# Float64 half units: one load shape and more staging slots, and the w_out remainder taken on VectorE

## The chip, the cores and the metric

The kernel runs on one core of a Trainium2 chip. The metric is the device time of one execution in microseconds (us); three executions of the kernel before took 1278.87, 1280.46 and 1280.32 us, median 1280.32 us.

## The reference

Three layers run one after the other, on 8 batches of 576 rows (4608 rows of 512 values):

```python
a = softmax(phi)                                   # 576 x 32 per head
k_m, v_m = einsum('bhsm,bhsd->bhmd', a, k), einsum('bhsm,bhsd->bhmd', a, v)
attn = softmax(q @ k_m.T / sqrt(64))
x = attn @ v_m                                     # layer 1, 4608 x 512
h = x @ moe_w_in                                   # layer 2, 512 -> 2048
x = (h * sigmoid(1.702 * h)) @ moe_w_out           # 2048 -> 512
e = argmax(x @ w_gate)                             # layer 3, one of 8 experts per row
out = gate * sigmoid(x @ w_output_gate)[e] * (relu(x @ w1[e]) @ w2[e])
```

The weights `moe_w_in` and `moe_w_out` arrive in float64. They are handed to the chip as their raw 64-bit words, and the kernel itself turns them into float32.

## The kernel before, in words

**Units and half units.** Layer 2's 2048 hidden values are cut into 16 units of 128. A unit has two half units of 128 rows by 512 float64 values (512 KB): one of `w_in`, one of `w_out`. There are `NV` = 32 half units. `conv_load(n)` brings half unit n into a staging tile on the SyncE queue (SP); it reads from the second byte pair on, so that the 16-bit pieces fall where the arithmetic wants them. Read so, the very last half unit would reach one piece past the end of the array. It is therefore loaded as 127 rows and one short row, by two DMAs (L181 and L183); the other 31 are one DMA of 128 rows each.

**Conversion.** `conv_slot(n)` converts half units n and n+1, so there are 16 conversions, those of `w_in` (n = 0, 4, ...) and of `w_out` (n = 2, 6, ...) in turn. Each is two ScalarE (ACT) calls (L195) that take the top pieces, then nine VectorE (DVE) instructions (L196 to L212) that put exponent and fraction together. For `w_out` the result is also split in two: ScalarE rounds it to fp32r (L214) and GpSimd (POOL) subtracts that from the value (L215), which leaves the remainder. Matmuls on TensorE (PE) are done three times with such pairs (`mm3`: high by high, high by low, low by high). For `w_in` the split comes later: `project` multiplies the unit by the attention's values on PE (L341), and ScalarE and VectorE split the product (L345, L346).

**Where half units wait.** Half units 0 to 11 land in four slots of the tile `wb` of weight group 2 (group 2's weights are converted later), the others in the pool `stg` with 3 buffers. `stg` also serves k and v of batches 2 to 7 and layer 3's weights. A load stands in SP's program behind the conversion that empties its slot.

**Steps.** The program is a list of steps: a step is one unit for one half batch (288 columns), that is 6 matmuls into `h`, the activation on ACT and DVE (L367 to L370), and 12 matmuls into four accumulators `acc`. The first 24 steps run units 0 to 5 for four half batches; each part sum goes to DRAM by `ev` (L387) and `partd` (L704). Then units 6 to 15 follow for the first half batch (steps 24 to 33), whose end is L393, where the part sum is added; by then all 16 conversions must be done. From there no weight of layer 2 is converted any more: the other half batches, layer 2 for batches 2 to 7, and layer 3 with its routing.

**Order.** Each engine runs its instructions in program order. Conversions are called at a fixed pace against the steps (`PB + j * PR`), or earlier where a step needs them; a scheduler then lays out each engine's order. The attention of batch 1 (`compress`, `query`) is spread over steps 0 to 12; its k and v lie in five chunks in `wb` of weight group 3, and its q is loaded by `load_q` on the same SP queue.

Of the kernel before, what the change touches and what calls it, by code (L numbers as in the profile page):

```python
# [10 lines left out]
F32 = mybir.dt.float32  # L11
F32R = mybir.dt.float32r
U32 = mybir.dt.uint32
I32 = mybir.dt.int32
U16 = mybir.dt.uint16
# [15 lines left out]
NF1, NF2 = 16, 8  # L31
SLOT = 128
# [5 lines left out]
OUT_SHAPE = (N, DM)  # L38
CH = [(0, 128), (128, 128), (256, 128), (384, 128), (512, 64)]
LOOK = 2  # L40
LEAD = 8
FE = 60
CV0 = (0, 4, 8)
NR, NT = 12, 24
O1, R1, OQ, RQ, OR, RR = 0, 0.5, 6, 0.4, 9, 0.6
S1 = 32
ORDER = 'p k0 k1 c0 k2 k3 c1 k4 q0 c2 w q1'
# [5 lines left out]
def tile_kernel(ctx: ExitStack, tc: tile.TileContext, phiT, kv, qT, w1, w2, wg, out):  # L53
    nc = tc.nc
    PS = bass.MemoryType.PSUM
    w1 = w1.bitcast(U16).rearrange("u a p n -> (u a p n)")

    const = ctx.enter_context(tc.tile_pool(name="const", bufs=1))
    sb = ctx.enter_context(tc.tile_pool(name="sb", bufs=2))
# [74 lines left out]
    def stage(g, slot, n=1024):  # L134
        a, b = group(g, "stage")
        t, o = (b, slot) if slot < 6 else (a, slot - 6)
        return t.rearrange("p u n -> p (u n)")[:, int(1024 * o):int(1024 * o) + n]
# [10 lines left out]
    def load_kv(b, c):  # L148
        s0, n = CH[c]
        if b < 2:  # L150
            t = stage(2, 6) if (b, c) == (0, 4) else stage(3, c)
        else:
            t = sb.tile([128, 1024], F32, name="stg", bufs=3)
        nc.sync.dma_start(out=t[:n], in_=kv[b, s0:s0 + n])
        kv_t[b, c] = t

# [11 lines left out]
    NV = 2 * NF1  # L168
    raw_t = {}
    loaded = [3]  # L170

    def conv_load(n):


        if n < NR:
            raw_t[n] = stage(2, 2 + n % 4).bitcast(U16)
        else:
            raw_t[n] = sb.tile([128, 2048], U16, name="stg", bufs=3)
        o = (2 * (2 * (n // 4) + n % 2) + n % 4 // 2) * 128 * 2048 + 1
        rows = 128 if n < NV - 1 else 127  # L180
        nc.sync.dma_start(out=raw_t[n][:rows], in_=w1[o:o + rows * 2048].rearrange("(p n) -> p n", p=rows))  # L181
        if rows < 128:
            nc.sync.dma_start(out=raw_t[n][rows:, :2047], in_=w1[o + rows * 2048:o + 128 * 2048 - 1].rearrange("(p n) -> p n", p=1))  # L183

    def conv_slot(n):


        if n < NT:
            top, t = (stage(3, 5 + (n + i) % 6 / 2, 512).bitcast(U16) for i in range(2))
        else:  # L190
            top, t = (sb.tile([128, 1024], U16, name=("phi0", "phi1", "c0")[(n + i) % 3], bufs=1) for i in range(2))
        raw = [raw_t.pop(n + i) for i in range(2)]
        tops = [x.rearrange("p (n b) -> p n b", b=4)[:, :, 2] for x in raw]
        for i in range(2):
            nc.scalar.activation(out=t.bitcast(BF16)[:, 512 * i:512 * i + 512], in_=tops[i].bitcast(BF16), func=AF.Abs)  # L195
        nc.vector.tensor_scalar(out=t.bitcast(BF16), in0=t.bitcast(BF16), scalar1=WLO, scalar2=WHI,  # L196
                                op0=ALU.max, op1=ALU.min)
        nc.vector.tensor_scalar(out=t, in0=t, scalar1=3, scalar2=0x3FFF,
                                op0=ALU.logical_shift_left, op1=ALU.bitwise_and)
        for i in range(2):  # L200
            h = slice(512 * i, 512 * i + 512)
            nc.vector.scalar_tensor_tensor(out=top[:, h], in0=tops[i], scalar=0xC000, in1=t[:, h],
                                           op0=ALU.bitwise_and, op1=ALU.bitwise_or)
        nc.vector.tensor_scalar(out=t, in0=top, scalar1=0xFF80, scalar2=None, op0=ALU.bitwise_and)
        for i in range(2):
            h = slice(512 * i, 512 * i + 512)
            u = 2 * (n // 4) + i
            wa, wb = (x[:, u % 4] for x in group(u // 4, "A"))
            m = raw[i].bitcast(U32).rearrange("p (n b) -> p n b", b=2)[:, :, 0]
            w = wa if n % 4 < 2 else m.bitcast(F32)  # L210
            nc.vector.scalar_tensor_tensor(out=w, in0=m, scalar=2.0 ** -36, in1=t.bitcast(BF16)[:, h], op0=ALU.mult, op1=ALU.mult)
            nc.vector.tensor_add(out=w, in0=w, in1=top.bitcast(BF16)[:, h])  # L212
            if n % 4 >= 2:
                nc.scalar.copy(out=wb[:, 512:1024], in_=w)  # L214
                nc.gpsimd.tensor_sub(out=wb[:, 1024:1536], in0=w, in1=wb[:, 512:1024].bitcast(F32))  # L215
                u_t[u] = (wb[:, 0:256], wb[:, 256:512]), (wb[:, 512:1024], wb[:, 1024:1536])
        while loaded[0] < min(NV, n + (6 if n + 5 < NR else 5)):
            conv_load(loaded[0])
            loaded[0] += 1

    d_reg = {}
    stg_t = {}

    def load2(key, src):
        stg_t[key] = sb.tile([128, 1024], F32, name="stg", bufs=3)
        nc.sync.dma_start(out=stg_t[key], in_=src)

    def split2(key, slot):
# [354 lines left out]
    def slot_tasks():  # L583
# [39 lines left out]
        def g(i):  # L623
            p = misc([128, 4, SLOT], 1 - i)
            for j in range(4):
                nc.tensor.transpose(p[:, j], st["h"][:, i, j], ident)
            t = sb.tile([128, 2, 4, SLOT], F32R, name="stg", bufs=3)
            nc.scalar.copy(out=t[:, 0], in_=p)
            nc.vector.tensor_sub(out=t[:, 1], in0=p, in1=t[:, 0].bitcast(F32))
            st["g", i] = t  # L630
# [50 lines left out]
    def spread(step, thunks, every=1):  # L681
        for i, t in enumerate(thunks):
            put(int(step + i * every), t)
# [50 lines left out]
    def attn_tasks():  # L734
        for b in range(B):
            s0 = S1 if b == 1 else start["A", b, 0]
            if b:
                q1 = query(b, 1)
                q1.insert(2, lambda b=b: load_q(b + 1, 0) if b + 1 < B else None)
                if b == 1:  # L740
                    spread(OR, q1, RR)
                else:
                    spread(s0 + 1, q1, 2)
            if b + 1 < B:
                n = b + 1
                cm = compress(n)
                q0 = query(n, 0)
                q0.insert(2, lambda n=n: load_q(n, 1))
                if b:
                    put(s0 + 1, lambda n=n: load_phi(n))  # L750
                    for c in range(3):
                        put(s0 + 2, lambda n=n, c=c: load_kv(n, c))
                    o = s0 + 8
                    put(o + 4, lambda n=n: load_kv(n, 3))
                    put(o + 5, lambda n=n: load_kv(n, 4))
                    spread(o, cm)
                    spread(o + 10, q0, 2)
                else:
                    put(O1, lambda n=n: load_phi(n), lambda n=n: load_q(n, 0))
                    for c in range(5):  # L760
                        put(O1, lambda n=n, c=c: load_kv(n, c))
                    spread(O1, cm, R1)
                    spread(O1 + OQ, q0, RQ)

    def project_tasks():
        place = {x[:4]: i for i, x in enumerate(steps)}
        for b in range(1, B):
            for u, n in ((0, 4), (4, 2), (6, 2), (8, 4), (12, 4)) if b == 1 and CUT % 4 else ((0, 4), (4, 4), (8, 4), (12, 4)):
                need, prev = place["A", b, 0, u] - LOOK, place["A", b - 1, 1, u + n - 1] - LOOK
                assert prev < need  # L770
                put(max(prev, need - LEAD), lambda b=b, u=u, n=n: project(b, u, n))

# [37 lines left out]
    done = [0]  # L810
# [33 lines left out]
    put(1, setup2)  # L844
    for i in range(-LOOK, n_steps):
        j = i + LOOK
        if j < n_steps:
# [29 lines left out]
def host(q, k, v, phi, moe_w_in, moe_w_out, moe2_w_gate, moe2_w_output_gate, moe2_w1, moe2_w2):  # L877
    import numpy as np
    c = np.ascontiguousarray
    phiT = c(phi.reshape(B, 2, 4, S, M).transpose(0, 1, 2, 4, 3).reshape(B, 2, 128, S))  # L880
    kvp = np.empty((B, S, H, 2 * D), np.float32)
    kt, vt = k.transpose(0, 2, 1, 3), v.transpose(0, 2, 1, 3)
    kvp[:, :, 0::2, :D] = vt[:, :, 0::2]
    kvp[:, :, 0::2, D:] = kt[:, :, 0::2]
    kvp[:, :, 1::2, :D] = kt[:, :, 1::2]
    kvp[:, :, 1::2, D:] = vt[:, :, 1::2]
    q6 = q.reshape(B, 4, 2, 2, HS, D)[:, :, ::-1]
    qTp = c(q6.transpose(0, 3, 2, 5, 1, 4).reshape(B, 2, 128, 4, HS))

    def units(wi, wo):  # L890
        f = wi.shape[1] // 128
        a = wi.reshape(KD, 128, f, 128).transpose(2, 1, 0, 3).reshape(f, 128, 512)
        return np.concatenate([a, wo.reshape(f, 128, 512)], axis=2)

    w1 = c(units(moe_w_in, moe_w_out).reshape(NF1, 128, 2, 512).transpose(0, 2, 1, 3)).view(np.int64)
    w2 = c(np.stack([units(moe2_w1[e], moe2_w2[e]) for e in range(E)]))
    wg = c(np.concatenate([moe2_w_gate, moe2_w_output_gate], axis=1).reshape(KD, 128, 16).transpose(1, 0, 2))
    return dict(phiT=phiT, kv=kvp.reshape(B, S, H * 2 * D), qT=qTp, w1=w1, w2=w2, wg=wg)
# [21 lines left out]
```

## Time and profile before

| | before |
|---|---|
| median of three executions | 1280.32 us |
| the profiled execution | 1287.78 us, span 1286.1 us |
| PE busy | 1196.4 us (93%) |
| DVE busy | 742.4 us (58%) |
| ACT busy | 497.7 us (39%) |
| POOL busy | 133.9 us (10%) |
| mean granted TensorE clock | 0.963 |

A share here is a mean over the whole span. The engines are limited by different things in the first 210 us, where weights are converted, and behind them, so the rows of each stretch are read apart.

### The profile page before, as it was taken

How to read it: one execution, taken by the hardware profiler on the slowest of the kernel's cores; microseconds unless marked ns; L12 is line 12 of the kernel's file. 1: busy time of each engine (PE TensorE's matmuls, PEld its weight loads, DVE VectorE, ACT ScalarE, POOL GpSimd, SP SyncE). 2: the span in 40 equal slices, each digit the busy share in tenths (PEclk: the TensorE clock that was granted, in tenths of full speed). 3: DMA queues.
4: the chain of work that ended last, by engine and by line, in shares of the span. 5: the costliest groups of instructions: out<-in, count | busy, mean ns of one | idle time of the engine just before them, and what ended most of it. 6: DMA issues, size and time to landing. Idle time of an engine off the chain costs nothing. (4 is left out here: it accounts for less than half of the span.)

```text
span 1286.1 us, 24689 instructions
## 1 busy us (share of the span) xinstructions
PE 1196.4 (93%) x9628; PEld 1107.5 (86%) x9628; DVE 742.4 (58%) x2011; ACT 497.7 (39%) x1144; POOL 133.9 (10%) x137
## 2 busy tenths in 40 slices
PE   4689737999999999999999999999999999999996
PEld 2478626888988988999889889989999999999995
DVE  5898726576466467466556546676463553544521
ACT  3445414344444444443443444553242332332410
POOL 1221000020100100101101102001110001001100
PEclk8689967999999999999999999999999999999998
DMA  8534313433311311401311310475453443534300
GB/s 297 193 107 122 131 63 95 126 80 88 108 42 56 112 39 56 130 20 56 130 38 38 119 31 20 107 230 150 130 162 95 136 156 85 171 103 123 116 23 22
DMA packets 77017, 132.00 MB, mean 103 GB/s; under 512 B 12738, under 2 KB 49730, under 8 KB 76898
## 3 DMA queue, kind: packets, MB, share of 16 engines
q1 hardware_dynamic: 75170, 130.25, 33.2%
q8 instruction: 76, 1.25, 0.4%
q14 instruction: 43, 0.35, 0.1%
q0 software_dynamic: 1728, 0.15, 0.1%
HBM read 99.65 MB, written 31.12 MB: 102 GB/s over the span
## 5 line engine op out<-in xcount | busy, mean ns | idle before, releaser
L352 PE MATMUL acc<-g,wb 128*128 128x288 f32 x4608 | 690.1, 298 | 13.5 <-ACT wb L214 6.2
L352 PEld LDWEIGHTS acc<-g,wb 128*128 128x128 f32 x4608 | 642.6, 191 | 22.1 <-ACT g L369 6.8
L352 PE MATMUL h<-x,wb 128*128 128x288 f32 x2560 | 478.0, 305 | 36.6 <-DVE g L370 24.2
L352 PEld LDWEIGHTS h<-x,wb 128*128 128x128 f32 x2560 | 386.4, 191 | 86.1 <-issue 30.7
L367 ACT ACTIVATE th<-h 128x288 f32<-128x288 f32 x256 | 105.0, 411 | 122.0 <-PE h L352 121.4
L352 PE MATMUL h<-x,wa 128*128 128x288 f32 x512 | 151.5, 296 | 0.0
L369 ACT CAST g<-th 128x288 fp32r<-128x288 f32 x196 | 84.9, 433 | 171.2 <-PE acc L352 149.0
L370 DVE TENSOR_TENSOR g<-th,g 128x288 fp32r<-128x288 f32 x196 | 88.8, 453 | 100.2 <-ACT g L369 99.9
L368 DVE SCALAR_TENSOR_TENSOR th<-th,h 128x288 f32<-128x288 f32 x196 | 87.8, 448 | 75.5 <-ACT th L367 74.6
L373 DVE SCALAR_TENSOR_TENSOR g<-h,g 128x288 fp32r<-128x288 f32 x128 | 58.0, 453 | 117.3 <-ACT g L372 116.9
L231 ACT CAST wb<-stg 128x1024 fp32r<-128x1024 f32 x72 | 75.6, 1050 | 105.5 <-PE acc L352 90.4
L372 ACT ACTIVATE g<-h 128x288 fp32r<-128x288 f32 x128 | 52.2, 408 | 162.9 <-PE acc L352 162.0
L352 PEld LDWEIGHTS h<-x,wa 128*128 128x128 f32 x512 | 96.8, 189 | 0.0
L232 DVE TENSOR_TENSOR wa<-stg,wb 128x512 fp32r<-128x512 f32 x72 | 51.5, 715 | 77.4 <-ACT wb L231 76.9
L578 POOL TENSOR_TENSOR rt<-rt,scl 128x1152 f32<-128x1152 f32 x15 | 33.6, 2241 | 352.5 <-DVE rt L404 252.4
L330 POOL TENSOR_TENSOR x<-sf,x 128x288 fp32r<-128x288 f32 x32 | 25.9, 808 | 420.7 <-ACT x L329 394.4
L514 POOL DMA_INDIRECT listd<-ids,pos x48 | 45.5, 948 | 188.8 <-DVE ssm L321 67.4
L233 DVE TENSOR_TENSOR wb<-stg,wb 128x512 fp32r<-128x512 f32 x72 | 57.0, 792 | 0.0
L341 PE MATMUL m<-wa,kvc 64*32 64x512 f32 (+1 forms) x592 | 42.2, 576 | 10.7 <-DVE wa L212 9.3
L346 DVE TENSOR_TENSOR wb<-m,wb 128x512 fp32r<-128x512 f32 (+1 forms) x74 | 42.3, 608 | 15.7 <-ACT wb L345 15.7
L345 ACT CAST wb<-m 128x512 fp32r<-128x512 f32 (+1 forms) x74 | 35.6, 529 | 17.9 <-PE m L341 17.7
L369 ACT CAST g<-h 128x288 fp32r<-128x288 f32 x60 | 23.9, 398 | 46.6 <-PE acc L352 30.0
(200 smaller groups left out, 811.1 us busy)
## 6 DMA issues: line engine op xcount, KB each, us to landing
stg<-in_w_dram SPq DMA_DIRECT2D x91, 512.0 KB, 4.0
stg<-in_kv_dram SPq DMA_DIRECT2D x24, 512.0 KB, 4.0
x2d<-x SPq DMA_DIRECT2D x16, 576.0 KB, 5.9
x2tok<-rt SPq DMA_DIRECT2D x64, 144.0 KB, 2.9
x<-x2d SPq DMA_DIRECT2D x16, 576.0 KB, 4.0
out_dram<-rt SPq DMA_DIRECT2D x64, 144.0 KB, 2.8
q<-in_qT_dram SPq DMA_DIRECT2D x15, 576.0 KB, 3.9
wb<-in_w_dram SPq DMA_DIRECT2D x12, 512.0 KB, 4.8
```

The lines of the kernel that those rows point to most:

```text
L231: nc.scalar.copy(out=wb[:, 0:1024], in_=stg)
L232: nc.vector.tensor_sub(out=wa, in0=stg[:, 0:512], in1=wb[:, 0:512].bitcast(F32))
L233: nc.vector.tensor_sub(out=wb[:, 1024:1536], in0=stg[:, 512:1024], in1=wb[:, 512:1024].bitcast(F32))
L346: nc.vector.tensor_sub(out=lo, in0=p[e], in1=hi.bitcast(F32))
L352: nc.tensor.matmul(p, lhsT=w[a][:, c0:c0 + 128], rhs=x[c], start=(first and i == 0), stop=(last and i == 2))
L367: nc.scalar.activation(out=t, in_=p, func=AF.Tanh, scale=0.851)
L368: nc.vector.scalar_tensor_tensor(out=o, in0=t, scalar=1.0, in1=p, op0=ALU.add, op1=ALU.mult)
L369: nc.scalar.copy(out=g[:, 0], in_=o)
L370: nc.vector.tensor_sub(out=g[:, 1], in0=o, in1=g[:, 0].bitcast(F32))
L372: nc.scalar.activation(out=g[:, 0], in_=p, func=AF.Relu)
L373: nc.vector.scalar_tensor_tensor(out=g[:, 1], in0=p, scalar=0.0, in1=g[:, 0].bitcast(F32), op0=ALU.max, op1=ALU.subtract)
L514: nc.gpsimd.indirect_dma_start(out=listd, out_offset=bass.IndirectOffsetOnAxis(ap=st["pos"][:, c:c + 1], axis=0), in_=ids[:, 2 * b * NJ + ...
```

## The change

The array is handed over flat and with one 64-bit word more at its end, so that the last half unit can be read as 128 rows by one DMA like the others. `stg` has 4 buffers in place of 3. Half units 12 to 15 land in the slots of group 2 as well, 16 to 19 in the four slots of group 3 in which k and v of batch 1 lay, and 20 to 31 in `stg`. Loads beyond half unit 15 are held until step 5 of the program (`free`), and then called for up to half unit 23 at once, later six ahead of the conversion. And the remainder of `w_out` (L215) is subtracted on VectorE.

```diff
+NS = 4
-NR, NT = 12, 24
+NR, NT = 16, 24
...
-            t = sb.tile([128, 1024], F32, name="stg", bufs=3)
+            t = sb.tile([128, 1024], F32, name="stg", bufs=NS)
...
         if n < NR:
             raw_t[n] = stage(2, 2 + n % 4).bitcast(U16)
+        elif n < NR + 4:
+            raw_t[n] = stage(3, n % 4).bitcast(U16)
         else:
-            raw_t[n] = sb.tile([128, 2048], U16, name="stg", bufs=3)
+            raw_t[n] = sb.tile([128, 2048], U16, name="stg", bufs=NS)
         o = (2 * (2 * (n // 4) + n % 2) + n % 4 // 2) * 128 * 2048 + 1
-        rows = 128 if n < NV - 1 else 127
-        nc.sync.dma_start(out=raw_t[n][:rows], in_=w1[o:o + rows * 2048].rearrange("(p n) -> p n", p=rows))
-        if rows < 128:
-            nc.sync.dma_start(out=raw_t[n][rows:, :2047], in_=w1[o + rows * 2048:o + 128 * 2048 - 1].rearrange("(p n) -> p n", p=1))
+        nc.sync.dma_start(out=raw_t[n], in_=w1[o:o + 128 * 2048].rearrange("(p n) -> p n", p=128))
...
                 nc.scalar.copy(out=wb[:, 512:1024], in_=w)
-                nc.gpsimd.tensor_sub(out=wb[:, 1024:1536], in0=w, in1=wb[:, 512:1024].bitcast(F32))
+                nc.vector.tensor_sub(out=wb[:, 1024:1536], in0=w, in1=wb[:, 512:1024].bitcast(F32))
...
-        while loaded[0] < min(NV, n + (6 if n + 5 < NR else 5)):
+        conv_loads(n + 6)
+
+    def conv_loads(n):
+
+        while loaded[0] < (min(NV, max(n, NR + 4 + NS)) if "free" in raw_t else min(n, NR)):
             conv_load(loaded[0])
             loaded[0] += 1
...
                     spread(O1, cm, R1)
+                    put(O1 + 5, lambda: raw_t.update(free=True), lambda: conv_loads(done[0] + 4))
                     spread(O1 + OQ, q0, RQ)
...
-    w1 = c(units(moe_w_in, moe_w_out).reshape(NF1, 128, 2, 512).transpose(0, 2, 1, 3)).view(np.int64)
+    w1 = units(moe_w_in, moe_w_out).reshape(NF1, 128, 2, 512).transpose(0, 2, 1, 3).reshape(-1)
+    w1 = np.concatenate([w1, w1[:1]]).view(np.int64)
```

In the order of the instructions the change shows at three places. Line numbers of the kernel after are up to 6 higher than those of before (L183 there is L181 here, L708 is L704, L155 is L154). On SP, the loads of half units 20 to 31 (`stg<-in_w_dram`) between the stores of the part sums (`partd`) stand so before:

```order
L181 DMA stg<-in_w_dram 128x2048 x4
L704 DMA partd_0_104<-ev 128x1152
L181 DMA stg<-in_w_dram 128x2048 x4
L704 DMA partd_1_105<-ev 128x1152
L181 DMA stg<-in_w_dram 128x2048 x4
L181 DMA stg<-in_w_dram 127x2048
L183 DMA stg<-in_w_dram 1x2047
L154 DMA stg<-in_kv_dram 128x1024
```

and so after:

```order
L708 DMA partd_1_103<-ev 128x1152
L708 DMA partd_0_104<-ev 128x1152
L183 DMA stg<-in_w_dram 128x2048 x4
L708 DMA partd_1_105<-ev 128x1152
L183 DMA stg<-in_w_dram 128x2048 x4
L155 DMA stg<-in_kv_dram 128x1024 x2
```

Behind the last part sum 4 loads are left in place of 5 and a short one, all of one shape; 8 stand behind the third part sum, where 9 and the short one stood.

On SP again, from the end of batch 1's k and v (`wb_119`, group 3) to batch 1's second q, the order was before (`wb_123` are the slots of group 2):

```order
L154 DMA wb_119<-in_kv_dram 64x1024
L120 DMA listd<-x_525 128x288
L181 DMA stg<-in_w_dram 128x2048 x2
L181 DMA wb_123<-in_w_dram 128x2048 x2
L181 DMA stg<-in_w_dram 128x2048 x3
L704 DMA partd_0_102<-ev 128x1152
L162 DMA q<-in_qT_dram 128x1152
```

and is after:

```order
L155 DMA wb_119<-in_kv_dram 64x1024
L121 DMA listd<-x_525 128x288
L183 DMA stg<-in_w_dram 128x2048 x3
L183 DMA wb_123<-in_w_dram 128x2048 x2
L183 DMA stg<-in_w_dram 128x2048
L183 DMA wb_123<-in_w_dram 128x2048 x2
L183 DMA wb_119<-in_w_dram 128x2048
L183 DMA wb_123<-in_w_dram 128x2048 x2
L183 DMA wb_119<-in_w_dram 128x2048 x3
L708 DMA partd_0_102<-ev 128x1152
L163 DMA q<-in_qT_dram 128x1152
```

Fourteen loads (half units 10 to 23) stand ahead of the first part sum's store and of that q, in place of seven (10 to 16); four of them go into the slots from which batch 1's k and v are read.

On DVE, the last conversion (half units 30 and 31) stood so before:

```order
L196 TENSOR_SCALAR phi_1719<-phi_1719 128x1024
L198 TENSOR_SCALAR phi_1719<-phi_1719 128x1024
L368 SCALAR_TENSOR_TENSOR h<-th,h 128x288
L202 SCALAR_TENSOR_TENSOR phi_1718<-stg,phi_1719 128x512 x2
L370 TENSOR_TENSOR g<-h,g 128x288
L204 TENSOR_SCALAR phi_1719<-phi_1718 128x1024
L368 SCALAR_TENSOR_TENSOR h<-th,h 128x288
L211 SCALAR_TENSOR_TENSOR stg<-stg,phi_1719 128x512 x2
L212 TENSOR_TENSOR stg<-stg,phi_1718 128x512 x2
L370 TENSOR_TENSOR g<-h,g 128x288
```

and stands so after (L372 and L374 there are L368 and L370 here, L350 is L346):

```order
L196 TENSOR_SCALAR phi_1710<-phi_1710 128x1024
L350 TENSOR_TENSOR wb_1439<-m_1726,wb_1439 128x2x128
L198 TENSOR_SCALAR phi_1710<-phi_1710 128x1024
L350 TENSOR_TENSOR wb_1439<-m_1727,wb_1439 128x2x128
L202 SCALAR_TENSOR_TENSOR phi_1709<-stg,phi_1710 128x512 x2
L372 SCALAR_TENSOR_TENSOR h<-th,h 128x288
L204 TENSOR_SCALAR phi_1710<-phi_1709 128x1024
L372 SCALAR_TENSOR_TENSOR h<-th,h 128x288
L211 SCALAR_TENSOR_TENSOR stg<-stg,phi_1710 128x512 x2
L212 TENSOR_TENSOR stg<-stg,phi_1709 128x512 x2
L374 TENSOR_TENSOR g<-h,g 128x288
L215 TENSOR_TENSOR wb_1439<-stg,wb_1439 128x512 x2
```

The two subtractions L215 follow the conversion with one other instruction between; seven more such pairs stand behind the other conversions of `w_out`.

## Rows read from the trace of the kernel before

**Rows 1.** The page: busy tenths of PE in 40 slices of the span.
```profile
PE   4689737999999999999999999999999999999996
```

**Rows 2.** Stretches: busy us of PE, PEld, DVE, ACT, POOL (instructions); clock, DMA share, GB/s.
```profile
17.00:146.00 129.00, 100.92 (x786) 81.41 (x787) 114.50 (x255) 61.05 (x146) 23.98 (x20) 0.81 0.46 157
146.00:208.00 62.00, 29.20 (x183) 24.88 (x182) 28.02 (x57) 15.10 (x34) 5.12 (x4) 0.70 0.30 96
208.00:1286.00 1078.00, 1058.79 (x8590) 997.45 (x8588) 595.81 (x1675) 415.63 (x954) 102.23 (x91) 1.00 0.32 94
...
174.00:196.00 22.00, 5.34 (x44) 3.38 (x44) 1.15 (x3) 1.55 (x4) 0.00 (x0) 0.58 0.13 48
```

**Rows 3.** Timeline: start, length, instruction [idle before it <- what ended that].
```profile
17.00 0.43 DVE L196 TENSOR_SCALAR wb<-wb 128x1024 bf16<-128x1024 bf16 x1 [7.34 <-ACT wb L195]
...
168.48 0.67 ACT L195 ACTIVATE c<-stg 128x512 bf16<-128x512 bf16 x1 [3.75 <-DMA stg<-in_w_dram]
...
195.76 0.65 ACT L195 ACTIVATE phi<-stg 128x512 bf16<-128x512 bf16 x1 [19.39 <-DMA stg<-in_w_dram]
196.45 0.43 DVE L196 TENSOR_SCALAR phi<-phi 128x1024 bf16<-128x1024 bf16 x1 [19.57 <-ACT phi L195]
...
199.33 1.09 PE L352 MATMUL h<-x,wb 128*128 128x288 f32 x3 [18.95 <-DVE g L370]
...
208.06 0.86 DVE L393 SCALAR_TENSOR_TENSOR x<-acc,x 128x288 f32<-128x288 f32 x2 [0.53 <-PE acc L352]
```

**Rows 4.** Timeline of SP's queue, the last weight loads.
```profile
172.65 0.31 SPq L181 DMA_DIRECT2D stg<-in_w_dram  x1
173.01 8.59 SPq L183 DMA_DIRECT2D stg<-in_w_dram  x1
```

**Rows 5.** DMA: rate in 40 slices of 184 to 195 us; issues, KB each, us to landing.
```profile
GB/s 328 209 60 30 30 30 15 30 30 15 30 30 30 15 30 30 30 15 30 30 30 15 30 30 15 30 30 30 15 30 30 30 15 30 30 15 30 30 30 15
...
stg<-in_w_dram SPq DMA_DIRECT2D x19, 512.0 KB, 5.2
```

**Rows 6.** DVE to 210 us by line and form: busy us, mean ns of one.
```profile
L323 DVE TENSOR_TENSOR sa<-sa,ssm 128x288 f32<-128x288 f32 x8 | 5.3, 684 | 0.0
...
L212 DVE TENSOR_TENSOR wa<-wa,wa 128x512 f32<-128x512 f32 x8 | 5.1, 682 | 0.0
...
L198 DVE TENSOR_SCALAR wa<-wa 128x1024 uint16<-128x1024 uint16 x8 | 5.0, 625 | 0.1
...
L313 DVE TENSOR_TENSOR sa<-sa,smx 128x288 f32<-128x288 f32 x8 | 3.3, 449 | 0.0
...
L211 DVE SCALAR_TENSOR_TENSOR wa<-wb,wa 128x512 f32<-128x512 uint32 x4 | 3.2, 836 | 0.0
...
L198 DVE TENSOR_SCALAR wb<-wb 128x1024 uint16<-128x1024 uint16 x4 | 1.7, 420 | 0.1
```

**Rows 7.** POOL to 215 us: busy us, mean ns of one, idle before it.
```profile
L215 POOL TENSOR_TENSOR wb<-stg,wb 128x512 fp32r<-128x512 f32 x10 | 13.3, 1350 | 91.7 <-ACT wb L214 91.7
L215 POOL TENSOR_TENSOR wb<-wb,wb 128x512 fp32r<-128x512 f32 x6 | 9.4, 1581 | 26.9 <-ACT wb L214 26.9
L330 POOL TENSOR_TENSOR x<-sf,x 128x288 fp32r<-128x288 f32 x8 | 6.4, 800 | 53.8 <-ACT x L329 27.6 <-DMA q<-in_qT_dram 26.2
```

**Rows 8.** Waits of DVE from 43 to 146 us: us in total, times, longest.
```profile
DVE h L368 <- ACT th L367: 6.4, 6, 2.7
DVE wa L196 <- ACT wa L195: 2.6, 2, 1.3
```

**Rows 9.** Timeline near 70 us, a remainder on ACT and POOL.
```profile
69.56 1.27 ACT L214 CAST wb<-wb 128x512 fp32r<-128x512 f32 x2 [2.21 <-DVE wb L212]
...
70.32 4.05 POOL L215 TENSOR_TENSOR wb<-wb,wb 128x512 fp32r<-128x512 f32 x2 [10.32 <-ACT wb L214]
```

**Rows 10.** Timelines of SP's queue and PE: batch 1's second q and its first use.
```profile
84.19 0.33 SPq L162 DMA_DIRECT2D q<-in_qT_dram  x1
...
92.53 0.72 PE L306 MATMUL m<-q,kvc 64*32 64x288 f32 x16
```

More of the change, by code (lines that the diff above doesn't have):

```diff
@@ L55, in tile_kernel @@
     PS = bass.MemoryType.PSUM
-    w1 = w1.bitcast(U16).rearrange("u a p n -> (u a p n)")
+    w1 = w1.bitcast(U16)
     const = ctx.enter_context(tc.tile_pool(name="const", bufs=1))
@@ L224, in load2 @@
     def load2(key, src):
-        stg_t[key] = sb.tile([128, 1024], F32, name="stg", bufs=3)
+        stg_t[key] = sb.tile([128, 1024], F32, name="stg", bufs=NS)
         nc.sync.dma_start(out=stg_t[key], in_=src)
@@ L626, in g @@
                 nc.tensor.transpose(p[:, j], st["h"][:, i, j], ident)
-            t = sb.tile([128, 2, 4, SLOT], F32R, name="stg", bufs=3)
+            t = sb.tile([128, 2, 4, SLOT], F32R, name="stg", bufs=NS)
             nc.scalar.copy(out=t[:, 0], in_=p)
```

## The prediction

> **What bounds the kernel now.** I read the page's slices first. PE is 90% busy or more from the eighth slice on, but not in the first seven, some 225 us, and slices five and six fall to 7 and 3 tenths [rows 1]. A cut by stretches says what each part hangs on [rows 2]. From the first conversion on DVE at 17.0 us [rows 3] to 146 us, DVE is busy for 114.5 of 129 us and PE for 100.9 at a mean clock of 0.81: that stretch is DVE's. From 146 to 208 us, where L393 ends the second pass over the first half batch [rows 3], both are idle for more than half of the time: PE 29.2 and DVE 28.0 of 62 us. From 208 us on PE is busy for 1058.8 of 1078 us at full clock, and nothing there is worth having for a change that ends with the conversions. So the question is when L393 runs. All later work follows it with PE as its bound, and the end moves as L393 moves.
>
> Why is the middle stretch empty? The timeline shows one chain [rows 3]: ACT's L195 sits idle for 19.39 us for a load into `stg`, DVE's L196 for 19.57 behind it, PE for 18.95 behind DVE. That load is the last half unit, issued at 172.65 us, its short row at 173.01 [rows 4]. From 186 to 195 us the transfer rate lies flat at 15 to 30 GB/s with nothing else moving; the 128-row loads of the same size have a median of 5.2 us from issue to landing [rows 5]. The 127-row load took 195.76 - 172.65 = 23.1 us. A smaller wait of 3.75 us, also for a load, stands in front of the conversion before [rows 3].
>
> **The change part by part.**
>
> *The last load as 128 rows.* At 5.2 us it would land at 172.65 + 5.2 = 177.9 us, not 195.8: 17.9 us off the chain, if nothing else moved.
>
> *More slots.* Before, loads 17 to 31 wait for `stg` slots one conversion at a time. After, eight loads are left behind the third part sum, the rest having been issued earlier, as the order shows. I expect ACT's L195 to wait for no load behind 43 us. That removes the 3.75 us above and DVE's 2.6 us between 43 and 146 us [rows 8]. At worst (slots come free no earlier than the loads are wanted) it removes nothing. Once L393 is past, the fourth buffer has nothing to win: PE is idle for 19.2 us in 1078 [rows 2]. The extra word of the array adds no instruction.
>
> *The remainder on DVE.* Sixteen subtractions of 128x512 are added to DVE. The nearest row is L212, the same shape, two operands in SBUF: 682 ns [rows 6], so 16 x 0.682 = 10.9 us. POOL loses 13.3 + 9.4 = 22.7 us [rows 7], which nobody waited for much. What DVE gets back is the stretch that POOL put on its instructions: L198 takes 625 ns on average in its first group and 420 in the second (8 x 0.205 = 1.6 us), L323 684 where its like L313 takes 449 (8 x 0.235 = 1.9), L211's slow group 836 against 682 (4 x 0.154 = 0.6): 4.1 us [rows 6]. L330 stays on POOL with 6.4 us, so I give L215 its share of POOL's time, 22.7 of 29.1: 3.2 us. Bounds: nothing, if the stretch is L330's, and 4.1.
>
> A page of the Trainium skill would give more: "SBUF — State Buffer", section "SBUF: two separate sides", says that GpSimd and VectorE share a pair of ports which one instruction holds alone, so that the other blocks, also where VectorE has two operands in SBUF. By it up to 22.7 us of DVE could come back and the subtractions would be free. The rows agree only in part: two L215 took 4.05 us near 70 us instead of twice 1.3 to 1.6 [rows 7, 9], so there POOL was the one that stood still.
>
> *A new wait.* DVE runs in order, and L215 needs ACT's rounding L214. The order puts one instruction of DVE between the conversion and L215. Two L214 take 1.27 us and begin as the first half is done [rows 9], so a pair of L215 can hold DVE for something between 0 and 1.27 us, eight times: 0 to 10 us. Queued behind it are L370, which PE's next 12 matmuls wait for, and the next conversion. L368 or the like covers some 0.4 us, and the first L214 starts early; I take 0.4 us a pair, 3 us.
>
> *The sum.* DVE's work from 17 to L393 was 114.5 + 28.0 = 142.5 us [rows 2]. After: 142.5 + 10.9 - 3.2 = 150.2. From 17 to 146 us DVE was idle for 14.5 us, 2.6 of it for loads [rows 8]; without these it was busy for 114.5 of 126.4 us, 90.6%. The rest of the idle time is the latency of ACT and PE (L368 for L367, 6.4 us, is the largest [rows 8]), and stays. 150.2 / 0.906 = 165.8, with the new wait 168.8 us, so L393 starts at 17.0 + 168.8 = 185.8 us instead of 208.1: 22.3 us less. A second way keeps the middle stretch's own pace: take out the waits for loads there (19.57 on DVE and the 3.75 us) and add 10.9 - 3.2 + 3 = 10.7 us of DVE, none of it hidden: 12.6 us; with half hidden in the idle time, 18. The first way lets the conversions fill DVE's idle time, which the order supports: the conversions of half units 22 to 29 stand one to three activations earlier than before. I take 21 us, nearer to the first. PE also ran at a mean clock of 0.70 in the middle stretch and at 0.58 from 174 to 196 us [rows 2]; with no long idle time it should be granted full speed, which is what lets PE follow DVE there.
>
> The profiled execution took 1287.8 us, 7.5 above the median of the three runs; I take the same 21 us off both: 1266.8 for a profiled execution and 1280.3 - 21 = 1259 us for the median. A change within 0.2% (2.6 us) can't be told from none.
>
> **The rivals.**
>
> *DVE is too full (gain of 3 to 14 us).* DVE is the bound to 146 us, and 10.9 us are put on it. If the full 10 us of waits for L214 come and all of the idle share stays (114.5 of 129, 88.8%): 150.2 / 0.888 + 10 = 179.1, L393 at 196.1, gain 12, so 1268 us. For it: POOL was all but idle. Against it: ACT is busy for 61.1 of 129 us [rows 2], so L214 seldom queues.
>
> The Trainium skill, "Perfetto Trace Analysis", section "Optimizing Scalar/DVE Operations", speaks for this rival: with VectorE saturated it advises to offload from it, even to GpSimd, though it adds that the shared port may spoil that. The trace agrees that DVE is saturated to 146 us (114.5 of 129 us).
>
> *PE alone is left (gain of 28 to 38 us).* If POOL's going frees much more of DVE than 3.2 us, the middle stretch falls to PE's work, 29.2 us in place of 62, gain 33: 1247 us. Against it: most conversions' rows lie at 680 to 690 ns even now, so little is there to free.
>
> *No effect (within 2.6 us).* The last load could stay slow for another reason than its 127 rows, its place at the array's end, say. Against it: rate and time are those of a transfer on few engines [rows 5], and the order shows it as 128x2048 like all others.
>
> On this the Trainium skill has a rule, "DMA: Bandwidth & Descriptors", section "Why a DMA increments its semaphore by 16 and not by 1": a transfer is split over the largest number of engines up to 16 that divides its outer size, so 127 rows go on one and 128 on sixteen. By that rule this rival is out, and the trace agrees as far as 15 to 30 GB/s can say.
>
> *SP's queue holds something back (slower than 1283 us).* Fourteen loads now stand before batch 1's second q, four of them into slots that batch 1's k and v must leave first. Before, this q was issued at 84.19 us and first used at 92.53 [rows 10], so with a landing of some 4 to 5 us it has about 4 us to spare. PE stands still behind a late q. To turn 21 us of gain into 2.6 of loss, q would have to come 4 + 23.6 = 28 us late; short of that it eats the gain. Against it: in PE's order the reads of that k and v stand before the last matmuls of the first part sum, whose store stood ahead of q before the change too.
>
> **How the numbers follow.** Forecast (gain of 14 to 28 us, 1252 to 1266): 0.68. DVE too full (1266 to 1277): 0.14. PE alone (1242 to 1252): 0.11. No effect: 0.03. Slower: 0.04. The likeliest is 1259 us. For 8 in 10 the range takes the forecast's and the near parts of its two neighbours: 1248 to 1270. Faster by over 0.2%: 0.68 + 0.14 + 0.11 = 0.93; same 0.03; slower 0.04.
>
> **What would show it.** In the profile after: no wait of ACT's L195 for `stg` above 2 us; L393 (L397 there) at 180 to 194 us; PE granted full clock from 150 to 190 us; L215 on DVE at 0.65 to 0.75 us each, and waits of L215 for L214 of 2 to 5 us in all; L198 and L323 near 0.43 us; the part behind L393 as long as before, within 3 us. I am wrong if the middle stretch is closed and the end does not move, if L215's waits reach 8 us, or if a wait for q or for a part sum has come up on PE.

## The result

The kernel after takes 1248.6 us (median of four executions, 1247.69 to 1249.97), the kernel before 1279.86 us in the four executions beside them. The ratio is 0.9757 (95% interval 0.9741 to 0.9774): 31.3 us faster, where 21 were forecast. The profiled execution took 1248.34 us, span 1246.6 us. L393 is L397 in the kernel after, and L195 to L215 keep their numbers.

The page of the kernel after, busy share and granted clock in 40 slices, against [rows 1]:

```profile
PE   4599889999999999999999999999999999999996
...
PEclk7689999999999999999999999999999999999998
```

The hole in slices five and six is gone, and from the fourth slice on the clock stands at nine tenths or more. By stretches (us from the start; busy us of PE, PEld, DVE, ACT, POOL with instructions; granted clock, DMA share, GB/s), the kernel before first, cut where the last copy of a part sum out of `acc` begins on DVE (142.88 us) and at L393:

```profile
17.00:142.88 125.88, 97.94 (x764) 78.43 (x764) 112.20 (x249) 59.10 (x142) 21.51 (x19) 0.81 0.47 159
17.00:208.06 191.06, 130.19 (x967) 106.35 (x968) 142.52 (x312) 76.21 (x180) 29.10 (x24) 0.78 0.41 137
208.06:1286.10 1078.04, 1058.73 (x8589) 997.39 (x8587) 595.81 (x1675) 415.57 (x954) 102.23 (x91) 1.00 0.32 94
```

The kernel after, cut at the same two events (139.41 and 172.53 us):

```profile
17.00:139.41 122.41, 96.44 (x745) 75.68 (x746) 116.18 (x265) 59.38 (x141) 7.08 (x8) 0.81 0.50 174
139.41:172.53 33.12, 27.91 (x223) 24.39 (x224) 29.98 (x65) 15.30 (x36) 0.00 (x0) 0.92 0.44 151
17.00:172.53 155.53, 124.35 (x967) 100.07 (x968) 146.16 (x328) 74.68 (x177) 7.08 (x8) 0.84 0.48 169
172.53:1246.60 1074.07, 1058.10 (x8589) 997.33 (x8587) 594.54 (x1676) 415.85 (x956) 103.01 (x91) 1.00 0.32 94
```

From 17 us to the end of the first half batch DVE is busy for 146.2 of 155.5 us (94%), before for 142.5 of 191.1 (75%). Its work grew by 3.6 us, its idle time fell from 48.5 to 9.4 us, and L397 starts 35.5 us earlier. DVE is still what that stretch waits for, not PE (124.4 us). What DVE waited for in it, us in total, times, longest; before:

```profile
DVE phi L196 <- ACT phi L195: 21.9, 3, 19.6
...
DVE h L368 <- ACT th L367: 6.8, 7, 2.7
DVE g L370 <- ACT g L369: 5.5, 9, 1.9
DVE c L196 <- ACT c L195: 5.3, 1, 5.3
DVE wb L346 <- ACT wb L345: 2.9, 3, 1.7
DVE wa L196 <- ACT wa L195: 2.6, 2, 1.3
```

and after:

```profile
DVE h L372 <- ACT th L371: 3.7, 9, 0.7
DVE g L374 <- ACT g L373: 2.2, 3, 1.0
DVE phi L196 <- ACT phi L195: 1.2, 2, 0.6
DVE wb L215 <- ACT wb L214: 0.8, 2, 0.5
...
DVE wb L350 <- ACT wb L349: 0.2, 1, 0.2
```

The wait for the first conversion, which ends at 17.0 us before and at 16.6 us after, is left out in both. Lines with L196 are conversions behind a late load, the others are latencies of ACT. The first fell from 29.8 us (21.9 + 5.3 + 2.6) to 1.2, and the second from 15.2 (6.8 + 5.5 + 2.9) to 6.9 with L215's new wait. DVE's instructions to 180 us by line and form, against [rows 6]:

```profile
L215 DVE TENSOR_TENSOR wb<-wb,wb 128x512 fp32r<-128x512 f32 x10 | 6.6, 687 | 0.3 <-ACT wb L214 0.3
...
L211 DVE SCALAR_TENSOR_TENSOR wb<-wb,wa 128x512 f32<-128x512 uint32 x6 | 4.5, 769 | 0.0
...
L215 DVE TENSOR_TENSOR wb<-stg,wb 128x512 fp32r<-128x512 f32 x6 | 3.9, 688 | 0.5 <-ACT wb L214 0.5
...
L327 DVE TENSOR_TENSOR sa<-sa,ssm 128x288 f32<-128x288 f32 x8 | 3.5, 453 | 0.0
L198 DVE TENSOR_SCALAR wa<-wa 128x1024 uint16<-128x1024 uint16 x8 | 3.4, 420 | 0.0
```

The subtraction takes 687 ns, L198 and L327 (L323 before) are back at 420 and 453 ns from 625 and 684.

### The profile page after: what moved, and what is told of

Its sections match the earlier page's. It is cut to its first block, busy times and chain, and to the rows that moved or that the text cites. A ratio compares the mean times of both kernels' runs of the same rounds, so it can differ in the third digit from the quotient of the medians.

```text
span 1246.6 us, 24653 instructions
## 1 busy us (share of the span) xinstructions
PE 1189.4 (95%) x9628; PEld 1101.0 (88%) x9628; DVE 745.2 (60%) x2027; ACT 496.5 (40%) x1144; POOL 112.6 (9%) x121
## 5 line engine op out<-in xcount | busy, mean ns | idle before, releaser
L374 DVE TENSOR_TENSOR g<-th,g 128x288 fp32r<-128x288 f32 x196 | 88.8, 453 | 99.5 <-ACT g L373 99.0
L372 DVE SCALAR_TENSOR_TENSOR th<-th,h 128x288 f32<-128x288 f32 x196 | 87.9, 448 | 75.4 <-ACT th L371 74.6
L350 DVE TENSOR_TENSOR wb<-m,wb 128x512 fp32r<-128x512 f32 (+1 forms) x74 | 42.7, 609 | 13.1 <-ACT wb L349 13.1
L345 PE MATMUL m<-wa,kvc 64*32 64x512 f32 (+1 forms) x592 | 41.4, 563 | 5.6 <-DVE wa L212 4.3
L349 ACT CAST wb<-m 128x512 fp32r<-128x512 f32 (+1 forms) x74 | 35.5, 528 | 20.9 <-PE m L345 20.9
## 6 DMA issues: line engine op xcount, KB each, us to landing
x2tok<-rt SPq DMA_DIRECT2D x64, 144.0 KB, 2.9
out_dram<-rt SPq DMA_DIRECT2D x64, 144.0 KB, 2.8
```

The costliest lines, as they stand in the source:

```text
L350: nc.vector.tensor_sub(out=lo, in0=p[e], in1=hi.bitcast(F32))
L372: nc.vector.scalar_tensor_tensor(out=o, in0=t, scalar=1.0, in1=p, op0=ALU.add, op1=ALU.mult)
L374: nc.vector.tensor_sub(out=g[:, 1], in0=o, in1=g[:, 0].bitcast(F32))
```

## The experiments

Theory A is the prediction's: the slow load, the slots and DVE's own work each carry a part, and the parts add up. Three rivals say where the excess of 10 us may lie. R1: the slots carry most of the gain. R2: POOL's leaving frees far more of DVE than was summed. R3: DVE no longer sets L397. Two more come up with the later runs: theory B (the last conversions wait because `stg` holds too few half units) and R4 (the slots of group 3 are what counts). "Rows" means the last load as 128 rows, "slots" all of the new landing places and the held-back loads, "sub" L215 on VectorE. The table has all times in us: medians, and the ratio to the kernel before on the same chip; the last row is a single execution. E is where the last copy of a part sum out of `acc` begins on DVE, X where L393 or its like begins, both in the profiled execution. A gain is the distance of a kernel's median to that of the kernel before on the same chip (1280.90 us for the first four kernels below the change's, 1280.26 for the next four, 1280.69 for the next three); two other kernels are compared by their medians, and where two gains are set against each other, by the difference of the gains.

| kernel | time | ratio (95%) | E | X |
|---|---|---|---|---|
| before | 1279.86 to 1280.90 | 1 | 142.9 | 208.1 |
| after (rows, slots, sub) | 1248.60 | 0.9757 (0.9741 to 0.9774) | 139.4 | 172.5 |
| before + rows | 1261.70 | 0.9841 (0.9818 to 0.9863) | 142.4 | 189.1 |
| before + sub | 1277.31 | 0.9977 (0.9966 to 0.9989) | 141.2 | 204.1 |
| before, last load cut 112 + 15 + 1 | 1265.52 | 0.9871 (0.9848 to 0.9893) | 144.0 | 192.2 |
| before + slots | 1264.54 | 0.9873 (0.9849 to 0.9896) | 138.8 | 189.5 |
| slots + sub | 1266.48 | 0.9894 (0.9857 to 0.9932) | 139.9 | 189.7 |
| rows + slots | 1247.53 | 0.9742 (0.9706 to 0.9777) | 139.5 | 170.9 |
| rows + sub | 1259.86 | 0.9843 (0.9810 to 0.9876) | 140.3 | 185.6 |
| after, each sub twice | 1263.39 | 0.9863 (0.9827 to 0.9899) | 153.0 | 189.9 |
| after, `evac` on ACT | 1244.81 | 0.9720 (0.9694 to 0.9745) | – | 171.3 |
| after, three `stg` buffers | 1255.61 | 0.9801 (0.9776 to 0.9827) | 138.3 | 181.8 |
| before + rows + four buffers | 1247.30 | 0.9750 (0.9721 to 0.9780) | 141.1 | 172.4 |
| before, profiled again | 1282.41 | – | 143.3 | 207.6 |

**Rows alone.** The kernel before with the longer array and the one DMA of 128 rows.

```diff
-        rows = 128 if n < NV - 1 else 127
-        nc.sync.dma_start(out=raw_t[n][:rows], ...)
-        if rows < 128:
-            nc.sync.dma_start(out=raw_t[n][rows:, :2047], ...)
+        nc.sync.dma_start(out=raw_t[n], in_=w1[o:o + 128 * 2048].rearrange("(p n) -> p n", p=128))
```

> Kernel before with the last half unit alone changed: one DMA of 128 rows, the array one word longer. Theory A (the slow last load is a stall of its own, and DVE sets the rest): the 19.4 us wait of ACT for that load goes to under 3 us, the other load waits stay, gain 16 to 20 us. Rival R1 (the missing slots are the cause, the last load only shows it): other load waits take its place, gain under 10 us.

1261.70 us, 19.2 less than the 1280.9 beside it. DVE's waits from E to X (lines three lower than in the kernel before):

```profile
DVE c L193 <- ACT c L192: 5.4, 1, 5.4
DVE phi L193 <- ACT phi L192: 4.0, 3, 2.5
```

The wait on the slow load is gone (the three waits of `phi` go from 21.9 to 4.0 us, which is 17.9 less), the one in front of it (`c`, 5.4 us) is as long as before. It doesn't move to another place: that is A, and not R1.

**The sub alone.** The kernel before with L215 on VectorE.

```diff
-                nc.gpsimd.tensor_sub(out=wb[:, 1024:1536], in0=w, ...)
+                nc.vector.tensor_sub(out=wb[:, 1024:1536], in0=w, ...)
```

> Kernel before with the remainder of w_out on VectorE alone. Theory A: 16 x 0.69 = 11 us more on DVE, some 4 us of stretch given back, and the last load hides behind it as before: 1 us faster to 6 us slower. Rival R2 (the subtraction on GpSimd holds DVE up by far more than its stretch): 8 us or more faster.

1277.31 us (11 executions), 3.6 us less than before by the medians, 2.9 by the ratio. That is far from the 8 us or more which R2 asked for, but also more than A allowed (1 us faster at best). DVE's work to X is 147.47 us against 142.52: 11 us of subtractions cost 5 us net.

**Is it the 127 rows?** The kernel before, its array as it was: the 127 rows are cut in two of 112 and 15, and the short row stays.

```diff
-        rows = 128 if n < NV - 1 else 127
-        nc.sync.dma_start(out=raw_t[n][:rows], ...)
+        cuts = (0, 128) if n < NV - 1 else (0, 112, 127)
+        for r0, r1 in zip(cuts, cuts[1:]):
+            nc.sync.dma_start(out=raw_t[n][r0:r1], ...)
```

> Kernel before with the 127 rows of the last half unit cut into two DMAs of 112 and 15 rows, the short row as before; the array as before. Theory A (the count of 127 rows makes the load slow): the same gain as with 128 rows in one DMA, within 1.5 us. Rival (its place at the array's end, or the short row, makes it slow): no gain.

1265.52 us: 15.4 us of the 19.2. The same bytes from the same place in the array now come in time; the timeline of ACT shows the last two conversions (lines one higher, each with the idle time before it where there was any):

```profile
174.85 0.67 ACT L196 ACTIVATE phi<-stg 128x512 bf16<-128x512 bf16 x1 [5.28 <-DVE wa L213]
180.10 0.65 ACT L196 ACTIVATE phi<-stg 128x512 bf16<-128x512 bf16 x1
```

The last one doesn't wait for its load at all, where before it sat idle for 19.39 us [rows 3]. So the shape of the DMA made it slow, not its place at the end. In the kernel before, the 127-row load moves 26 GB/s while it runs alone, and the mean busy share of the 16 DMA engines is 0.06, as much as one engine of 16 at work all the time (1/16 = 0.0625):

```profile
187.00:194.00 7.00, 0.00 (x0) 0.00 (x0) 0.00 (x0) 0.00 (x0) 0.00 (x0) 0.50 0.06 26
```

By the Trainium skill's rule on the split of a transfer ("DMA: Bandwidth & Descriptors", section "Why a DMA increments its semaphore by 16 and not by 1"), 112 rows go on 16 engines, 15 rows on 15, and 127 rows on one. The share of 0.06 and the time of the cut load agree with it.

The kernel is 3.8 us slower than with the one DMA, more than the 1.5 us expected. It isn't the load: DVE's waits for `phi` are 1.4 us here, 4.0 with the one DMA. X comes 3.1 us later, with 1.9 us more work on DVE and 1.2 us more idle time; what causes that is open.

**Slots alone.** The kernel after with the array, the load and L215 of before.

> Kernel before with the slots, the fourth buffer and the held-back loads alone; the last load still 127 rows and a short one, the remainder on GpSimd. Theory A: the last load is issued some 10 us ahead of its use and takes 23, so a stall of 10 to 15 us stays; gain 8 to 14 us. Rival R1: gain 20 us or more.

1264.54 us, 16.4 less than before: a little over A's 8 to 14, under R1's 20. The slots do almost nothing for DVE's wait on the slow load (19.6 to 17.9 us), though its short row is issued at 153.1 us instead of 173.0, and take away nearly everything else. DVE's waits from 17 us to X (lines up to 7 higher than in the kernel before):

```profile
DVE phi L199 <- ACT phi L198: 18.5, 2, 17.9
...
DVE h L375 <- ACT th L374: 5.7, 7, 2.4
DVE g L377 <- ACT g L376: 2.1, 5, 0.5
...
DVE wb L353 <- ACT wb L352: 0.2, 1, 0.2
```

All waits for loads fell by 11.3 us (29.8 to 18.5), 9.6 of it those other than the slow one (10.2 to 0.6), and those for ACT by 7.2 (15.2 to 8.0). Together that is 18.5 us, and X is 18.6 us earlier.

**Everything but the rows.** The kernel after with the 127 rows and the short row.

> Kernel after with the last half unit loaded as before (127 rows and a short row). Theory A: a stall of 10 to 15 us comes back, so 1258 to 1264 us. Rival R1 (slots are what counts): within 4 us of the kernel after, 1252 or less.

1266.48 us, a gain of 13.8 of the 31.3: the slow load alone is worth 17.5 us of the change, and stands again as a wait of DVE of 17.2 us. A's 1258 to 1264 us was 2.5 us too low, and R1's 1252 or less is out.

**Everything but the sub.** The kernel after with L215 on POOL.

> Kernel after with the remainder of w_out back on GpSimd. Theory A (DVE sets L393 and gains 4 us of stretch for 11 us of work): 2 to 7 us faster than the kernel after, 1242 to 1247. Rival R2 (the subtraction on GpSimd holds up DVE, or PE waits for it): 3 us or more slower than the kernel after.

1247.53 us, no difference from the kernel after that can be told (0.9742 and 0.9757, intervals that overlap), where A had it 2 to 7 us faster. The forms on DVE from 17 to 215 us show why (this kernel has the line numbers of the kernel after):

```profile
L198 DVE TENSOR_SCALAR wa<-wa 128x1024 uint16<-128x1024 uint16 x8 | 5.7, 709 | 0.0
...
L211 DVE SCALAR_TENSOR_TENSOR wb<-wb,wa 128x512 f32<-128x512 uint32 x6 | 5.0, 866 | 0.0
L327 DVE TENSOR_TENSOR sa<-sa,ssm 128x288 f32<-128x288 f32 x8 | 4.8, 614 | 0.0
```

With POOL at work beside it, DVE's own instructions are longer again (L198 709 ns against 420). DVE is busy for 143.03 us to X with L215 on POOL and for 146.16 with it on DVE: of 11.0 us that come, 7.9 are given back. The stretch with L215 on POOL:

```profile
17.00:170.91 153.91, 118.37 (x968) 96.39 (x969) 143.03 (x312) 75.42 (x180) 28.18 (x24) 0.86 0.49 169
```

So R2's mechanism is there, but it about pays for the subtractions and leaves no gain. The Trainium skill's page "SBUF — State Buffer", section "SBUF: two separate sides", allowed up to the whole of POOL's time, 22.7 us here [rows 7]; the four pairs of kernels with L215 on one engine or the other give 5.8 to 8.7 us. In the two pairs at the ends of that range the records up to X hold 13 instructions more and not 16, so these two figures are some 1 to 1.5 us too high.

**Everything but the slots.** The kernel before with rows and sub.

> Kernel before with the 128-row load and the remainder on VectorE, but the old slots and three buffers. Theory A: load waits of DVE of some 8 us in all come back: 1254 to 1260 us. Rival R1: 1262 or more.

1259.86 us. Rows and sub alone bring 20.4 us, which is what A expected and R1 denied; the missing 11 us are the slots. DVE's waits for loads to X are 8.6 us, A's "some 8".

**DVE's work by itself.** The kernel after, with each L215 issued a second time: 16 more instructions and 11 us more on DVE.

> Kernel after with each of the 16 subtractions on VectorE done twice, the second to the same place with the same result: 11 us more of DVE work and nothing else. Theory A (DVE sets L393): 8 to 12 us slower than the kernel after. Rival R3 (PE sets it by now, DVE has room): under 3 us slower.

1263.39 us, 14.8 more, and X is 17.3 us later. DVE's stretch and its longest waits in it:

```profile
17.00:189.85 172.85, 134.47 (x958) 109.67 (x958) 155.00 (x343) 74.80 (x179) 7.43 (x8) 0.87 0.42 151
...
DVE h L373 <- ACT th L372: 8.5, 9, 3.0
DVE g L375 <- ACT g L374: 5.1, 5, 1.7
```

R3 falls: DVE still sets L397, and work put on it costs its full length and some more. A's 8 to 12 us were too few. Of the 17.3 us, 8.8 are more work on DVE (155.00 against 146.16; 15 of the 16 new instructions are in the records) and 8.5 more idle time (17.9 against 9.4), most of it the two waits for ACT shown (3.7 and 2.2 us in the kernel after). So DVE's idle time is no constant here either; why it grew wasn't tried.

**DVE's work taken away.** The kernel after, with the two of four `evac` copies (`x` or part sum out of `acc`, 288 columns) that ran on DVE moved to ACT.

```diff
     def evac(dst, scale):
         for d in range(KD):
-            if d % 2:
+            if d % 2 and scale != 0.5:
```

> Kernel after with all four evacuations of an accumulator on ScalarE instead of two on VectorE: in the conversions' stretch 8 x 0.45 = 3.6 us less on DVE, as much more on ACT. Theory A (DVE sets L393): 2 to 5 us faster than the kernel after, 1244 to 1247 us. Rival R3 (PE and the order set it): within 1.5 us of the kernel after.

1244.81 us, the fastest median of all, with an interval that just touches that of the kernel after (0.9694 to 0.9745 against 0.9741 to 0.9774). To L397 eight instructions have left DVE; 24 more have left it behind L397, where the part takes as long as before (1074.2 and 1074.1 us):

```profile
17.00:171.31 154.31, 122.79 (x967) 99.47 (x968) 144.00 (x320) 77.71 (x185) 7.28 (x8) 0.86 0.49 170
```

Its work is 2.2 us less (144.00 against 146.16) and X comes 1.2 us earlier; the span is shorter by as much (1245.5 against 1246.6). The profile thus accounts for 1 us of the 3.8 between the medians. That the version beats the kernel before is shown; that it beats the kernel after is likely and not settled.

**Which of the slots?** The kernel after with `NS = 3`, all else kept (the loads called for at step 5 then go up to half unit 22).

> Kernel after with three buffers of stg; the slots of groups 2 and 3 and the early loads stay. Theory B (the last conversions wait for loads because stg holds only one and a half of them): 6 to 14 us slower than the kernel after, 1255 to 1263. Rival R4 (the slots of group 3, which load 20 half units before the second pass, are what counts): within 3 us of the kernel after.

1255.61 us, 7.0 more: that is B, and not R4's under 3. Of the slots' 11 us the fourth buffer is worth the larger part. Without it waits for loads are back between E and X:

```profile
DVE phi L196 <- ACT phi L195: 4.4, 3, 2.5
DVE c L196 <- ACT c L195: 2.0, 1, 2.0
```

A conversion takes two half units, so three buffers hold one and a half.

**The small version.** The kernel before with rows, four buffers, and loads always six half units ahead; no slots of group 3, half units 12 to 15 in `stg`, nothing held back, L215 on POOL.

> Kernel before with the 128-row load, four buffers of stg and loads six ahead throughout; no slots of group 3, the remainder on GpSimd. Theory B: 6 to 14 us faster than the 128-row load alone, 1247 to 1256. Rival R4: within 3 us of the 128-row load alone, 1259 or more.

1247.30 us: as fast as the whole change. DVE's waits from E to X (lines three lower than in the kernel before):

```profile
DVE phi L193 <- ACT phi L192: 1.3, 2, 0.6
DVE pmx L246 <- DMA phi<-in_phiT_dram: 1.1, 2, 0.8
```

No wait for a half unit above 0.6 us is left. So the landing places in `wb` and the held-back loads add nothing to the fourth buffer that can be measured (1247.53 us with them, L215 on POOL in both). Loads six ahead go with the fourth buffer here, where the kernel before had five; with three buffers they still leave waits for loads (1255.61 us), and four buffers with five ahead were not tried.

**The kernel before, profiled again.** To see how much of its first profile was chance.

> The kernel before once more, for a second profiled execution: the first took 1287.8 us, above all its timed runs. Theory A: near 1280 us, with L393 some 4 us earlier than at 208.1 and the part behind it some 4 us shorter; the wait for the last load 19 us again. Rival: 1287 us again, so the profile itself costs that much.

1282.41 us. The stretches, cut at E and X:

```profile
17.00:143.33 126.33, 97.92 (x764) 78.42 (x764) 112.83 (x248) 58.44 (x142) 21.52 (x19) 0.93 0.46 157
143.33:207.63 64.30, 32.88 (x203) 28.40 (x203) 30.33 (x65) 17.57 (x40) 7.64 (x6) 0.66 0.29 96
```

X is where it was, within 0.4 us, and not 4 us earlier as expected. Of the 5.4 us by which the first profiled execution was longer, 5.0 lay behind L393: 1078.0 us there, 1073.1 here (1280.7 - 207.6).

## Why the prediction was right in its kind and too small in its size

31.3 us fall into the range, but only just: 1248.6 us is 0.6 us from its end, so that the number fell in is partly luck. The slow load, the slots and DVE's work each count, as the prediction said; the terms of its sum that were off are named below. The forecast's own stretch (14 to 28 us) was left on the side of the rival with PE alone, but not by that rival's way: DVE is busy for 94% up to L397, and 11 us more on it cost 14.8.

- **The last load as 128 rows, 17.9 us: right.** DVE's waits for `phi` fell by 17.9 us, the time by 19.2 alone and by 17.5 on top of the rest. The rival "no effect" falls with the cut into 112 and 15 rows.
- **The step that failed: "The rest of the idle time is the latency of ACT and PE, [...] and stays."** I kept 15.6 us of idle time (150.2 / 0.906 - 150.2) and added 3 for L215. Measured were 9.4 us in all. The kernel with the slots alone shows where it went: waits for L367, L369 and L345 fell from 15.2 to 8.0 us, with rows alone only to 13.7 (6.9 + 5.7 + 1.1 in the first kernel above). Rows and four buffers alone, L215 still on POOL, have 8.9 us, and the subtractions alone 11.7. How the slots do it wasn't tried apart. Either DVE has a conversion ready to run in the meantime, or ACT, which runs in order, no longer stands at L195 with L367 queued behind it. The trace of the kernel before shows one wait of the second kind (130 us, below): DVE stands 1.28 us for L367, which stood behind an L195 that had waited 2.95 us for a load. Its longest wait for L367 (2.67 us) had PE in front of it instead.
- **The slots, "3.75 us above and DVE's 2.6 us": mis-sized.** Alone they are worth 16.4 us of time, on top of rows and sub 10.9. Of DVE's waits for loads they removed 11.3 us, not 6.4: the 3.75 us were ACT's, and DVE stood for 5.3 behind it; two more short waits of `phi` were not counted (1.7), and 1.7 came off the slow load's own.
- **The stretch given back, 3.2 us with 4.1 as upper bound: too small.** The subtractions cost 0.687 us each, as priced (0.682). But DVE's work to L397 is 146.2 us and not 150.2; the four pairs give 5.8 to 8.7 us back, the ends being some 1 to 1.5 us too high as said. I had summed three lines of [rows 6]. With L215 back on POOL in the kernel after, others are longer too: L202's slowest group takes 830 ns against 686, L317 516 against 451.
- **The wait of L215 for L214, 3 us: too large.** It was 0.8 us in all, in two waits. This makes 2.2 us of the 9.2 us of idle time below.
- **The sum.** L397 was forecast at 185.8 and came at 172.5 us, outside the 180 to 194 given. 4.0 of these 13.3 us are work (150.2 - 146.2), 9.2 idle time (18.6 - 9.4).
- **The part behind L393: as long as before.** 1074.1 us against 1078.0, so 3.9 us where I allowed 3; the second profile of before has 1073.1, and over all kernels here the profiled executions lie between 1071.2 and 1078.0. So this part differs by more than I allowed, by 5.0 us between two executions of one kernel. The 39.4 us between the two first profiles therefore overstate the change: some 5 of the 7.5 us of the profiled execution above the median were chance behind L393. L397 came 35.5 us earlier (35.1 against the second profile) and the median 31.3; the rest of that difference is open.
- **DVE too full; SP's queue.** Neither came. In the kernel after, PE has no wait for q up to L397, and its one wait there for a DMA is 2.0 us for k or v, where the kernel before had 1.5.
- **The other signs.** ACT's L195 waits for `stg` at most 0.6 us at a time up to L397, as forecast. The clock granted to PE from 150 to 190 us is 0.96 in the mean, with 0.66 from 160 to 165, and not full throughout. One reading was loose: of the first seven slices the fourth too stands at nine tenths [rows 1]; nothing hangs on it.

The waits for ACT with rows and four buffers alone, from 17 us to X (lines three lower than in the kernel before):

```profile
DVE h L365 <- ACT th L364: 4.7, 5, 2.0
DVE g L367 <- ACT g L366: 4.0, 9, 1.1
...
DVE wb L343 <- ACT wb L342: 0.2, 1, 0.2
```

In the kernel before, a wait for ACT behind a load, first ACT and then DVE:

```profile
130.01 0.66 ACT L195 ACTIVATE wa<-stg 128x512 bf16<-128x512 bf16 x1 [2.95 <-DMA stg<-in_w_dram]
130.57 0.40 ACT L367 ACTIVATE th<-h 128x288 f32<-128x288 f32 x1
...
131.00 0.46 DVE L368 SCALAR_TENSOR_TENSOR h<-th,h 128x288 f32<-128x288 f32 x1 [1.28 <-ACT th L367]
```

By time the parts nearly add up: rows 19.2 and slots 16.4 make 35.6 and bring 32.7 together. The sub, 3.6 by itself, brings nothing where the slots are in place (1247.53 us without it, 1248.60 with; slots alone 1264.54, slots and sub 1266.48). The profiles show where the difference lies. Without the slots, the subtractions add 5.0 and 5.2 us of work on DVE up to X, and its idle time falls by 8.9 and 8.7 us (48.5 to 39.6, and 29.7 to 21.0 with rows). With the slots they add 3.1 and 2.3 us, and the idle time falls by only 1.5 and 2.1 us (10.9 to 9.4, and 29.4 to 27.3 without rows). So the subtractions gained where they took up idle time that the slots take up too; which wait each of them fills no kernel showed by itself.

## What to carry to other kernels

Look at the shape of a slow DMA before its place or its size: one row more or a cut made a 23 us load an ordinary one. Count staging buffers in portions of what the consumer takes at once; here a consumer of two lost 7.0 us with three buffers against four, and more landing places behind that were worth nothing that could be measured. And when waits for loads go from an engine that runs near its limit, don't keep its old busy share: here the small waits of the same stretch went with them, and DVE was busy for 94% where 90.6% had been carried over.

## What the runs showed that was not expected

**The clock granted early did not matter in the kernel before.** In the two profiles of the kernel before TensorE was granted 0.81 and 0.93 of full speed from 17 us to E, and that stretch took 125.9 and 126.3 us, with PE busy for 97.9 us in both. DVE set its pace, with 112.2 and 112.8 us of work.

**Moving work off POOL and putting it on DVE cost next to nothing.** 11.0 us of subtractions added only 2.3 to 5.2 us to DVE's busy time in the four pairs (by an estimate 3 to 6, if the three instructions missing in two of the pairs are allowed for), because other instructions became shorter (from the kernel with L215 on POOL to the kernel after): L198 by 289 ns of 709, L327 by 161 of 614. In time the four moves came to between 3.6 us faster and 2.6 us slower.
